# Sorted block attention and Fourier feed-forward: a trip through DRAM for mixed V, row stores without waits, norms by ln and exp, unread matmuls

## The chip, the cores and the metric

One core of a Trainium2 chip runs the whole program. The metric is the device time of one execution in microseconds. The kernel before takes 292.82 us (median of 3 runs, 292.41 to 292.87).

Five engines matter here: TensorE (PE in the profile), VectorE (DVE), ScalarE (ACT), GpSimd (POOL) and SyncE (SP, which here issues transfers only). Sixteen DMA engines move data beside them.

## The reference, cut to what matters

```python
def _attn_ref(q, k, v, sort_net):            # q, k, v: 4 x 8 x 768 x 64
    P = sort_net                             # 4 x 8 x 8 x 8
    for _ in range(5):
        P = np.exp(P - max); P = P / rowsum; P = P / columnsum
    k_sorted = einsum('bhij,bhjcd->bhicd', P, k_b)   # blocks of 96 keys are mixed
    v_sorted = einsum('bhij,bhjcd->bhicd', P, v_b)
    attn = softmax over the keys of a block of (q_b @ k_sorted.T / 8)
    return attn @ v_sorted

def _moe_ref(x, w1, w2):                     # x: 4 x 768 x 512
    u = x + real(fft2(x))
    un = (u - mean) / sqrt(var + 1e-6)
    return u + relu(un @ w1) @ w2            # 512 -> 2048 -> 512
```

V has to be mixed between blocks (contraction over block and head, 128 rows at a time) and must then lie with keys on partitions for attention times V. That turn is what the change does in another way.

## The kernel before

The kernel is written as a list of operations with costs, which a planner puts in a fixed order for each engine before the program is built. Two halves of V (t = 0 for batches 0 and 1, t = 1 for 2 and 3) go through the same code. V is loaded in long pieces, summed over keys on PE, reordered on VectorE and ScalarE into `vcx`, mixed by 64 small matmuls per half, whose output already has keys on partitions, and evicted with a stride into `vsf`:

```python
load(nat[t] ..., vv[128 * t:128 * t + 128, 48 * hf:48 * hf + 48, :])   # 6144 B pieces
... nc.tensor.matmul(psm.ap, idh, nat[t][:, ...512 columns])           # 12: sum over keys
... copy(e, vcd[:, dr, :, 8 * hf:8 * hf + 8], src)                     # 8 reorderings
for dd in range(4):
    nc.tensor.matmul(o, vcx[:, 96 * d:96 * d + m], bd, ...)            # keys x (block, head)
copy(e, vsb[0:96, :, 4 * n:4 * n + 4], ps...)                          # 16 strided evictions
```

Residual rows `u` live in six buffers of 128 x 512. A buffer is free again only when the store of its rows has landed. Rows of the first half of a sequence are stored by SP, the others by GpSimd with an indirect store:

```python
if T < 2:
    nc.sync.dma_start(out[b, t0:t0 + 128, :], u.ap)
elif T == 2:                                   # three stores: 112 rows, 15 rows, row 0
    ...
else:
    nc.gpsimd.indirect_dma_start(out..., rows[:, i:i + 1], u.ap)
```

The softmax here doesn't subtract the row's maximum and nothing guards it: scores larger than these inputs give would overflow.

Of the kernel before, what the change touches and what calls it, by code (L numbers as in the profile page):

```python
# [27 lines left out]
LOOK = {}  # L28
QB = (2, 3)
# [14 lines left out]
GT = 384  # L44


def _consts():
# [56 lines left out]
    vrow = np.zeros((1, 128, D + 1), f16)  # L104
# [9 lines left out]
    def as32(m):  # L114
# [8 lines left out]
                rows=rows, erow=np.tile(erow, (1, 4)), vrow=vrow, pack=pack)  # L123


class Op:
    __slots__ = ("n", "costs", "fn", "preds", "succs", "left", "ready", "prio",
                 "vts", "fresh", "nbytes", "end", "start", "eng", "tag",
                 "crit", "late")
# [13 lines left out]
class Plan:  # L143
# [14 lines left out]
    def add(self, costs, fn, r=(), w=(), prio=None, nbytes=0, tag="",  # L158
            after=()):
# [7 lines left out]
        o.preds, o.succs, o.vts, o.fresh = set(after), [], [], []  # L167
        for k in r:
            o.preds.update(self.wr.get(k, ()))
# [41 lines left out]
    def schedule(self):  # L211
# [48 lines left out]
        while todo:  # L260
# [70 lines left out]
            for s in o.succs:  # L331
                s.left -= 1
                for x in s.costs:
                    s.ready[x] = max(s.ready[x],
                                     o.end + (0.03 if x == e else self.XL))
                if s.left == 0:
                    for x in s.costs:
                        avail[x].append(s)
# [27 lines left out]
def kernel(  # L366
# [22 lines left out]
    def many(name, n, shape, dtype):  # L389
# [18 lines left out]
    vcx = ct("vcx", [128, 128 * D + 2], F16)  # L408
    dtab = vcx[:, 6144:7168].rearrange("p (c w) -> p c w", c=4)
    lt = vcx[0:97, 7168:7168 + LTW]  # L410
    vsf = ct("vsf", [97, 128 * (D + 1)], F16)
    vsb = vsf[:, 0:128 * (D + 1)].rearrange("p (g w) -> p g w", w=D + 1)
    eb4 = ct("eb4", [97, 4, EW], F16)
    P.pool("eb", [eb4[:, n, :] for n in range(4)])
# [14 lines left out]
    many("un", 2, [128, DM], F16)  # L429
# [9 lines left out]
             vcx[:, 7938:8194].bitcast(F32).rearrange(  # L439
# [3 lines left out]
    vbn = ct("vbn", [128, D], F16)  # L443
    rows = ct("rows", [128, 3 * B], mybir.dt.uint32)
    negone = ct("negone", [128, 1], F32)
    mhalf = ct("mhalf", [128, 3], F32)
    mone = ct("mone", [128, 3], F32)
# [7 lines left out]
    pk = hr[1].rearrange("p a b -> p (a b)")[0:32, 0:1024].rearrange(  # L455
        "p (i x) -> p i x", i=NB)
    pv = hr[1].rearrange("p a b -> p (a b)")[0:32, 1024:3072].bitcast(
        F32).rearrange("p (i x) -> p i x", i=NB)
    pws = hr[1].rearrange("p a b -> p (a b)")[0:32, 3072:3232].bitcast(F32)
# [9 lines left out]
    def load(dst, src, nbytes, w, prio, eng="POOL", r=(), after=()):  # L469
        e = {"POOL": nc.gpsimd, "SP": nc.sync}[eng]  # L470
        c = (0.8, 0.8) if eng == "POOL" else (0.1, 2.3)
        o = P.add({eng: c}, lambda _: e.dma_start(dst, src), r=r, w=w,  # L472
                  prio=prio, nbytes=nbytes, tag="load", after=after)
        o.late = 4.0 if after else 0.0
        return o


    slot = {}
# [34 lines left out]
    def load_v(t, hf, prio):  # L513
        load(nat[t].rearrange("p (c d) -> p c d", d=D)[
            :, 48 * hf:48 * hf + 48, :],
            vv[128 * t:128 * t + 128, 48 * hf:48 * hf + 48, :], 1572864,
            [("nat", t, hf)] + (hk(0)[8 * hf:8 * hf + 8] if t == 0 else
                                kqk(2 * hf) + kqk(2 * hf + 1)), prio)
# [10 lines left out]
    for n in range(4):  # L529
        P.add({"POOL": (1.5, 1.6)}, lambda _, n=n: nc.gpsimd.memset(  # L530
            eb4[0:96, n, :], 0.0), w=[("ebz", n)], prio=-190.0, tag="ebz")
# [8 lines left out]
    for t_, val in ((negone, -1.0), (mhalf, -0.5), (mone, 1.0)):  # L540
        P.add({"POOL": (0.1, 0.4)}, lambda _, t_=t_, val=val:
              nc.gpsimd.memset(t_, val), w=["smalls"], prio=-199.0, tag="small")
    P.add({"POOL": (0.9, 0.9)}, lambda _: nc.gpsimd.tensor_tensor(
        mone, mone, mhalf, op=ALU.pow), r=["smalls"], w=["mone"], prio=-198.0,
        tag="small")
# [5 lines left out]
            "o (n s) -> o n s", n=4), 13376),  # L551
        vrow=(vsf[96:97, 0:128 * (D + 1)], cn["vrow"].ap(), 16640),
# [14 lines left out]
    load_qk("k", 0, 0, -5000.0)  # L567
    load_qk("q", 0, 0, -4999.0)
    load_v(0, 0, -4998.0)
    load_v(0, 1, -4997.0)  # L570
    load_qk("k", 0, 1, -4996.0)
    load_qk("q", 0, 1, -4995.0)
    load_c("dtab", -4994.0)
    load_c("lt", -4993.0)
    load_c("cs", 19.0)
    load_c("tab", 20.0)
    for c in range(4):
        load_w1(c, 40.0 + c)
    for hf in range(2):
        load_qk("k", 1, hf, 30.0 + hf)  # L580
        load_qk("q", 1, hf, 30.5 + hf)
    for c in range(4):
        load_w2(c, 50.0 + c)
# [4 lines left out]
    V = nc.vector  # L588

    exps = []  # L590

    def sk(c, fn):
        o = P.add(c, fn, r=["pw", "rs"] + hk(1), w=["pw", "rs"], tag="sink")
# [3 lines left out]
    for it in range(5):  # L597
# [16 lines left out]
        sk({"DVE": (0.21, 0.21)}, lambda _: V.tensor_tensor(  # L614
# [6 lines left out]
        r=["pw"], w=["pk"] + hk(1), tag="pk")  # L621
    P.add({"ACT": (1.0, 1.05)}, lambda _: nc.scalar.copy(
        pv.rearrange("p i (g j) -> p i g j", j=NB),
        pw[:, :, None, :].broadcast_to([32, NB, 16, NB])),
        r=["pw"], w=["pv"] + hk(1), tag="pv")
# [6 lines left out]
    P.add(pe(0.45), f, r=["pk", "pack"] + hk(1), w=[bk], tag="psk")  # L632
# [35 lines left out]
    def v_path(t):  # L668
        n3 = nat[t].rearrange("p (c d) -> p c d", d=D)
        psm = Buf("pm", "pf") if t else Buf("pm")  # L670
        stage = [i for n in range(4) for i in kqk(n)] if t else hk(0)
        for hf in range(2):
            def f(_, hf=hf):
                for n in range(6):
                    nc.tensor.matmul(
                        psm.ap, idh,
                        nat[t][:, 3072 * hf + 512 * n:3072 * hf + 512 * n
                               + 512], start=(hf == 0 and n == 0),
                        stop=(hf == 1 and n == 5))
            P.add(pe(mm(512, 6) * (1.0 if t else 1.2)), f,  # L680
                  r=[("nat", t, hf), "pack"] + (
                      stage if t else stage[8 * hf:8 * hf + 8]), w=[psm], tag="psm")
        P.add({"DVE": (0.6, 0.68)}, lambda _: V.tensor_reduce(
            vb[:, 0, :], psm.ap.rearrange("p (c d) -> p d c", d=D),
            axis=AX.X, op=ALU.add), r=[psm], w=["vb"], tag="vb")
# [8 lines left out]
        vcd = vcx[:, 0:6144].rearrange("p (d r c) -> p d r c", r=6, c=16)  # L694
        for n in range(8):
            qd, hf = divmod(n, 2)
            dr = slice(16 * qd, 16 * qd + 16)
            src = n3[:, 48 * hf:48 * hf + 48, dr].rearrange(
                "p (c r) d -> p d r c", r=6)
            dst = vcd[:, dr, :, 8 * hf:8 * hf + 8]  # L700
            if t == 0:
                P.add({"DVE": dve(768), "ACT": act(768, 0.75)},
                      lambda e, dst=dst, src=src: copy(e, dst, src),
                      r=[("nat", 0, hf)] + stage[8 * hf:8 * hf + 8],
                      w=[("vcx", n)], tag="vcp")
            else:
                P.add({"DVE": dve(768, 1.0, 0.55)},
                      lambda _, dst=dst, src=src, dr=dr: V.tensor_tensor(  # L708
                          dst, src, vbn[:, dr, None, None].broadcast_to(
# [672 lines left out]
```

## Time and profile before

| what | before |
|---|---|
| median time | 292.82 us |
| span of the profiled run | 290.0 us |
| first feed-forward matmul (the hand-over) | 70.25 us |
| end of the last matmul | 281.46 us |
| tail after it | 8.5 us |
| mean granted clock of PE (the share of full speed that PE's clock was given) | 0.981 |

Up to the hand-over VectorE is full and PE waits; after it PE is full. The prediction below shows the lines. The timeline columns are start, duration, engine, line, operation, output and input.

```profile
7.52 6.17 POOL L530 MEMSET eb<- 96x1672 f16 x4
...
15.03 0.67 DVE L618 CAST hr<-hr 32x1024 f16<-32x1024 f32 x1
```

GpSimd's zero fills of the exponentials' buffers end at 13.69, and VectorE's conversion of the permutation comes after them, at 15.03, and takes 0.67 us. The second is from the DMA part: packets of all queues by size, then one group of transfers (how many, size of each, median time from issue to landing):

```profile
DMA packets 42529, 26.33 MB, mean 91 GB/s; under 512 B 30106, under 2 KB 38824, under 8 KB 42500
...
kq<-in_v_dram POOLq DMA_DIRECT2D x2, 768.0 KB, 21.5
```

The second half of V comes in two transfers.

### The profile page before, as it was taken

The numbers are of one execution on the slowest core, as the hardware profiler recorded it, in microseconds if no ns is written. First come the engines' busy times: TensorE is split into PE (matmuls) and PEld (weight loads), VectorE is DVE, ScalarE is ACT, GpSimd is POOL, SyncE is SP. The second block draws the span as 40 slices with busy tenths as digits, with TensorE's granted clock in tenths as the row PEclk, the third lists the DMA queues.
The fourth block names the chain that finished last, engine by engine and source line by source line (L and its number), as shares of the span: only waits on it lengthen the run. The fifth ranks groups of instructions, "written<-read, shape, count | busy, mean of one in ns | idle before, by whom it ended". The sixth has DMA issues, their size and how long they took to land.

```text
span 290.0 us, 5807 instructions
## 1 busy us (share of the span) xinstructions
PE 260.9 (90%) x2284; PEld 155.2 (54%) x2284; DVE 171.9 (59%) x405; ACT 157.9 (54%) x323; POOL 66.3 (23%) x104
## 2 busy tenths in 40 slices
PE   0389988897999999999999999999999999999980
PEld 0258866554565656554566456455555546545530
DVE  4697999999999999831579643145034226210020
ACT  2677979785778945970477037137415505425300
POOL 8973300015900640011220002032000212200021
PEclk9997999998899999999999999999999999999997
DMA  7999999910990897211113010311311111221001
GB/s 114 211 260 245 215 208 211 219 37 5 157 146 10 95 165 133 66 37 20 77 47 57 36 52 22 58 72 50 57 72 37 38 54 72 38 90 36 2 36 72
DMA packets 42529, 26.33 MB, mean 91 GB/s; under 512 B 30106, under 2 KB 38824, under 8 KB 42500
## 3 DMA queue, kind: packets, MB, share of 16 engines
q0 software_dynamic: 23536, 18.31, 37.4%
q1 hardware_dynamic: 18966, 7.64, 11.6%
q8 instruction: 18, 0.29, 0.4%
q14 instruction: 9, 0.07, 0.1%
HBM read 28.96 MB, written 6.29 MB: 122 GB/s over the span
## 4 chain that ended last, share of the span: by engine, by line
PE 62%; DVE 22%; DMA 8%; issue 3%; POOL 2%; ACT 1%; POOLq 0%; DVEq 0%
PE bank L1253 26%; PE bank L1274 25%; DMA hr<-in_v_dram 4%; DVE vsf L660 3%; DVE vcx L708 3%; DVE rt L1006 3%; DMA out_dram<-u,rows 2%; POOL kq L472 2%; DMA kq<-in_q_dram 2%; PE bank L1149 2%; PE bank L991 2%; DVE st L1186 1%; PE bank L952 1%; PE bank L897 1%; DVE ks L660 1%
## 5 line engine op out<-in xcount | busy, mean ns | idle before, releaser
L1265 ACT ACTIVATE hr<-bank 128x384 f16<-128x384 f32 x115 | 56.3, 491 | 75.2 <-PE bank L1253 74.4
L1253 PE MATMUL bank<-ut,w1sb 128*128 128x384 f16 x512 | 92.8, 329 | 0.7 <-ACT ut L660 0.7
L1274 PE MATMUL bank<-w2sb,hr 128*128 128x512 f16 x384 | 87.9, 379 | 0.0
L1253 PEld LDWEIGHTS <-w1sb 128*128 128x128 f16 x512 | 49.0, 99 | 34.8 <-issue 1.8
L1274 PEld LDWEIGHTS <-hr 128*128 128x128 f16 x384 | 36.7, 98 | 41.8 <-issue 0.2
L1282 DVE TENSOR_TENSOR u<-bank,u 128x512 f32<-128x512 f32 x24 | 16.5, 689 | 60.2 <-PE bank L1274 59.8
L961 ACT ACTIVATE ex<-bank 96x384 f32<-96x384 f32 x64 | 27.9, 485 | 6.3 <-PE bank L952 6.0
L1295 POOL DMA_INDIRECT out_dram<-u,rows x12 | 12.2, 1013 | 77.0 <-DVE u L1282 56.7
L1193 POOL TENSOR_SCALAR mv<-mv 128x3 f32<-128x3 f32 x8 | 1.9, 240 | 109.8 <-DVE mv L1188 109.8
L976 ACT ACTIVATE eb<-ex,negone 96x384 f16<-96x384 f32 x35 | 20.8, 615 | 0.2
L1213 ACT ACTIVATE un<-u,nm,ny 128x512 f16<-128x512 f32 x15 | 12.2, 810 | 11.8 <-DMA ut<-un 8.5
L1172 DVE SCALAR_TENSOR_TENSOR u<-rt,bank 128x510 f32<-128x510 f16 x12 | 8.1, 678 | 16.3 <-PE bank L1138 8.9
L991 PE MATMUL bank<-vsf,eb 97*128 97x65 f16 x416 | 16.5, 193 | 1.3 <-DVE rr L836 0.5
L1006 DVE TENSOR_TENSOR rt<-bank,rz 128x384 f16<-128x384 f32 x32 | 17.2, 549 | 0.3
L991 PEld LDWEIGHTS <-eb 97*128 97x128 f16 x416 | 15.4, 98 | 3.6 <-issue 1.3
L472 POOL DMA_DIRECT2D kq<-in_q_dram x20 | 16.4, 850 | 1.7 <-DMA kq<-in_q_dram 1.2
L1186 DVE BATCH_NORM_STATS2 st<-u 128x6 f32<-128x512 f32 x24 | 16.1, 686 | 0.3
L1160 DVE SCALAR_TENSOR_TENSOR u<-rt,bank 128x512 f32<-128x512 f16 x12 | 8.0, 684 | 13.9 <-PE bank L1153 13.5
L927 PE MATMUL bank<-pack,qr 128*128 128x128 f16 x48 | 4.8, 246 | 12.3 <-ACT qr L660 11.7
L724 PE MATMUL bank<-bdv,vcx 128*128 128x128 f16 (+1 forms) x128 | 12.6, 225 | 0.0
L952 PE MATMUL bank<-qt,ks 64*128 64x96 f16 x256 | 11.3, 207 | 1.3 <-DVE rt L1006 0.4
L897 PE MATMUL bank<-bdk,kq 128*64 128x128 f16 x192 | 10.7, 228 | 1.6 <-DVE bdk L636 0.8
(130 smaller groups left out, 338.2 us busy)
## 6 DMA issues: line engine op xcount, KB each, us to landing
kq<-in_k_dram POOLq DMA_DIRECT2D x8, 384.0 KB, 6.6
w1sb<-in_moe_w_ch_dram POOLq DMA_DIRECT2D x4, 512.0 KB, 16.0
w2sb<-in_moe_w_ch_dram POOLq DMA_DIRECT2D x4, 512.0 KB, 19.0
out_dram<-u SPq DMA_DIRECT2D x8, 256.0 KB, 2.0
kq<-in_q_dram POOLq DMA_DIRECT2D x4, 384.0 KB, 11.6
hr<-in_v_dram POOLq DMA_DIRECT2D x2, 768.0 KB, 11.2
kq<-in_v_dram POOLq DMA_DIRECT2D x2, 768.0 KB, 21.5
kq<-in_q_dram POOLq DMA_DIRECT2D x16, 96.0 KB, 5.5
```

Source lines behind the costliest of these rows:

```text
L472: o = P.add({eng: c}, lambda _: e.dma_start(dst, src), r=r, w=w, prio=prio, nbytes=nbytes, tag="load", after=after)
L897: nc.tensor.matmul(ps.ap[64 * h2:64 * h2 + 64, 128 * r3:128 * r3 + 128], k16[:, 2 * hl + h2, 3 * half + r3, :], bdk[:, 2 * hp + h2].rearra ...
L952: nc.tensor.matmul(pss[h2].ap[:, BLK * j:BLK * j + BLK], ks.ap[rows, 4 * g + j, :], qt.ap[rows, c0:c0 + BLK])
L961: nc.scalar.activation(ex.ap, pss[h2].ap[0:96, 0:384], AF.Exp, scale=SCALE),
L976: nc.scalar.activation(ed, src, AF.Identity, bias=negone[0:96])
L991: nc.tensor.matmul(po.ap[:, 65 * T:65 * T + 65], eb.ap[:, e0:e0 + 128], vsf[:, vi:vi + 65], start=(n == 0), stop=(n == len(WIN[T]) - 1), s ...
L1006: P.add({"DVE": (0.45, 0.56)}, lambda _: V.tensor_tensor(rt.ap[:, :, D * h:D * h + D], po3()[:, :, 0:D], rz.ap[:, :, None].broadcast_to([1 ...
L1186: P.add({"DVE": (0.6, 0.69)}, lambda _, u=u, st=st: V.bn_stats(st.ap, u.ap), r=[u], w=[st], tag="bn")
L1253: nc.tensor.matmul(ps.ap[:, 0:GT], w1sb[:, c, 128 * fc:128 * fc + 128], ut.ap[:, c, :], start=(c == 0), stop=(c == 3))
L1265: nc.scalar.activation(hr[g][:, fc, :], ps.ap[:, 0:GT], AF.Relu)
L1274: nc.tensor.matmul(ps.ap, hr[g][:, fc, 128 * tt:128 * tt + 128], w2sb[:, fc, :], start=(fc == 0), stop=(fc == 15))
L1282: V.tensor_tensor(u.ap, ps.ap, u.ap, op=ALU.add),
```

## The change

The intent: free VectorE and ScalarE before the hand-over (V needs no reordering and no strided eviction if a DMA does the turn), shorten the tail, keep PE's clock up with matmuls whose results nobody reads (unread matmuls). The core of the diff, cut:

```diff
 def load_v(t, hf, prio):            # second half of V
+        for r in range(3 * hf, 3 * hf + 3):
+            load(nat[1][:, 1024 * r:1024 * r + 1024].rearrange("p (c d) -> p c d", d=D),
+                vv[128:256].rearrange("p (c r) d -> p r c d", r=6)[:, r], ...)
 def v_path(t):                      # its sum moves from PE to VectorE
+        if t:
+            for n in range(4):
+                V.tensor_reduce(vb[:, 0, 16 * n:16 * n + 16],
+                    n3.rearrange("p c d -> p d c")[:, 16 * n:16 * n + 16], ...)   # planned 1.65 us
 def v_mix(t):                       # 12 wide matmuls, contiguous evictions, trip through DRAM
-                    nc.tensor.matmul(o, vcx[:, 96 * d:96 * d + m], bd, ...)
-                      e, vsb[0:96, :, 4 * n:4 * n + 4], ...
+                nc.tensor.matmul(o, bd, n4[:, r, 8 * hf:8 * hf + 8], ...)
+                      e, vm[:, 512 * n:512 * n + 512], ps.ap
+        for hb in range(2):
+            for k_ in range(3):
+                ....dma_start(vdr[t][w64, cols], vm[w64, cols])                   # 256 KB store
+                nc.gpsimd.dma_start(vsb[32 * k_:32 * k_ + 32, w64, 0:D],
+                    vdr[t][w64, cols].rearrange("g (c d) -> c g d", d=D))         # gather
 # exponentials: six buffers instead of four
+    for n in range(NEB):
+        P.add({"DVE": (1.0, 1.1)} if n < 2 else {"POOL": (1.5, 1.6)}, ... memset(eb4[0:96, n, :], 0.0))
 # norms: 1/sqrt by ln and exp on ScalarE instead of a chain on GpSimd (cut)
 # row stores
+                for x in st_:
+                    for y in stores if T < 3 else stores + direct:
+                        tc.declare_no_dep(x.ins, y.ins, reason="each row stored once")
 # unread matmuls in PE's planned gaps up to the hand-over
+                    for _ in range(int((o.start - t - 0.05) / SPIN)):
+                        nc.tensor.matmul(spin.ap[:, 0:480], idh, pack.bitcast(F16))
-    load_c("tab", 20.0)
+    load_c("tab", ...)              # ahead of K of batch 1
```

The order of many other operations changes too, because everything is planned anew.

## The prediction

> **What bounds the kernel now.** I read the busy shares in 40 slices first, then the chain that ended last, then stretches of ten and two microseconds, then the last ten microseconds by instruction.
>
> ```profile
> PE   0389988897999999999999999999999999999980
> DVE  4697999999999999831579643145034226210020
> PEclk9997999998899999999999999999999999999997
> ```
>
> DVE is full in slices 4 to 16 (about 30 to 115 us), PE from about 70 us to 280. The two clock dips, near 22 and 72 us, matter below.
>
> ```profile
> 3.55 12.80 DMA hr<-in_v_dram
> ...
> 20.05 0.36 PE bank L897 x6
> ...
> 31.11 2.75 DVE vsf L660 x4
> ...
> 69.61 0.59 ACT ut L660
> 70.25 2.14 PE bank L1253 x8
> ```
>
> The chain (start, duration, what) waits for V until 16.4 us, then goes through DVE and ACT evictions until the first feed-forward matmul at 70.25. I call that point the hand-over. After it I counted PE's instructions from 110 to 282 us and multiplied by warm spacings read off the chain (4 of L1253 in 0.65 us, 4 of L1274 in 0.86, 26 of L991 in 0.80, 4 of L1149 in 0.44): 448 x 0.1625 + 344 x 0.216 + about 23 us of smaller groups = 170 us of work in 172. The same count over 70.25 to 110 gives some 39 us in 39.75. So after the hand-over PE is the bound, and the span is three terms: hand-over (70.25) + PE's remaining work (211.2, to 281.46) + tail (8.5).
>
> ```profile
> 22.00:24.00 2.00, 2.00 (x28) 1.66 (x29) 1.79 (x5) 1.83 (x7) 1.07 (x3) 0.78 1.10 323
> 24.00:26.00 2.00, 2.00 (x26) 1.46 (x24) 1.30 (x4) 0.98 (x2) 0.53 (x1) 0.50 1.31 203
> 40.00:50.00 10.00, 7.91 (x160) 6.35 (x159) 9.97 (x28) 9.57 (x22) 0.00 (x0) 1.00 1.21 207
> 70.00:72.00 2.00, 1.75 (x8) 0.99 (x8) 1.87 (x6) 1.23 (x3) 1.85 (x4) 0.72 0.00 0
> 72.00:74.00 2.00, 2.00 (x12) 1.16 (x10) 1.67 (x3) 1.27 (x4) 2.00 (x3) 0.50 0.57 52
> ```
>
> Each row: stretch, length, busy PE, PEld, DVE, ACT, POOL, then granted clock, DMA share, GB/s. From 40 to 50 us both evicting engines are full (9.97 and 9.57 of 10). The clock is down at 22 to 26, while V is mixed, and again right at the hand-over.
>
> ```profile
> 278.12 0.69 DVE L1282 TENSOR_TENSOR u<-bank,u 128x512 f32<-128x512 f32 x1 [0.19 <-PE bank L1274]
> 278.22 1.09 POOL L1295 DMA_INDIRECT out_dram<-u,rows  x1 [29.14 <-DVE u L1282]
> 281.57 0.69 DVE L1282 TENSOR_TENSOR u<-bank,u 128x512 f32<-128x512 f32 x1 [2.76 <-PE bank L1274]
> 281.86 0.97 POOL L1295 DMA_INDIRECT out_dram<-u,rows  x1 [2.55 <-DMA out_dram<-u,rows]
> 285.36 0.96 POOL L1295 DMA_INDIRECT out_dram<-u,rows  x1 [2.52 <-DMA out_dram<-u,rows]
> ```
>
> The second and third row stores of the last group are each held until the one before has landed; their data were ready at 278.81 and 282.26.
>
> **What the Trainium skill says.** *TensorE: Matmul & The Clock Gate*, Part 1 (the HAM clock gate): the array runs at 1.2 GHz after about one idle window of 3.4 us and at 2.4 GHz after a busy one. The trace agrees: the first six matmuls that sum V take 2.77 us together, the next six 1.46, and the stretch at 24 us has clock 0.50. *DMA: Bandwidth & Descriptors*, Anatomy of one DMA: about 2.0 us fixed per transfer; here an indirect store lands a median 2.7 us after issue. The same page, Specifications: line rate needs pieces of at least 512 B; the gather of mixed V moves 128 B pieces, which nothing in this trace times. *ScalarE: Activation LUTs*, Table sets: exp and ln share the set natural_log_exp_and_others, one load. The trace has one table load of 1.28 us; that no second appears is for the changed profile to show.
>
> **The change, part by part.**
>
> *Mixed V, first half (before the hand-over).* Removed: eight reorderings of V (5 on DVE of 941 ns, 3 on ACT of 1499: 9.2 us) and 16 strided evictions (774 to 791 ns; 11.5 us of the 23.0 in both halves). Added: 12 contiguous evictions of 512 columns. ACT's copy of 128x512 from PSUM took 586 ns and DVE's 64x512 cast 684, so 12 x 0.63 = 7.6 us. Added also: two memsets moved from POOL to DVE (my estimate 1.4 us, from 336 ns for a 768-column f16 copy) and a second expansion of the permutation (1.04, as L622 took). Net 10.7 us less on two engines that are both full: 5.3 us each. PE loses 128 small matmuls and gets 24 of 512 columns; at 22 to 28 us it was on the chain with clocks of 0.78, 0.50 and 0.87, a loss of 2 x (0.22 + 0.50 + 0.13) = 1.7 us which the unread matmuls should save. Together 7.0 us.
>
> A check by the other road, the arrival of mixed V. V goes first: 3.15 of the 4.7 MB that had come by 16.37 us, so 3.55 + 12.8 x 0.67 = 12.1 us. Sum, mean and bdv then end near 15, PE and evictions near 20.5. Store (2.3 to 3 us), then three gathers. If a 128 B piece costs what the plan of the change assumes (1.7 us per gather), V is back near 29 us, against 35 now (last eviction at 34.20, 0.79 long). That is 6 us, consistent with 7. The batch-0 scores, exponentials and their evictions (about 24 us on two engines) fill the wait, and six instead of four buffers for exponentials let them.
>
> *Norms by ln and exp.* The POOL chain from 64.33 to the first normalised row at 66.21 is 1.9 us, on the chain. Two small ACT operations and one DVE operation I put at 0.7 with their hops. Gain 1.2 us. The seven later norms lie beside full PE: nothing.
>
> *Unread matmuls up to the hand-over.* Keep the clock up at 70 to 74 us, where PE has just become the bound: 2 x 0.28 + 2 x 0.50 = 1.5 us.
>
> *Mixed V, second half.* DVE loses 8 x 1.473 us, PE trades 64 x 0.055 for 12 x 0.216: 0.9 us off PE's remaining work. The relief of DVE (some 7 us of both engines together) lies beside a full PE.
>
> *Stores without waits.* The third store starts at 282.3 instead of 285.36: 3.1 us off the tail. Elsewhere the waits (10.1 us of POOL, 5.5 of DVE for u buffers) are beside PE.
>
> *Loads moved.* The row-bias table is small and its consumer is fed before the hand-over anyway: 0.
>
> *Paid back.* Before 70.25 the present kernel has also done all of batch 1's attention on PE, about 9 us (96 / 2 x 0.0485 + 128 / 2 x 0.035 + 104 x 0.031 + 24 x 0.055). With an earlier hand-over part is left for later. But the same work costs 15 us per evicting engine, so leaving it also brings the hand-over forward; I book 0.5 us net loss.
>
> Sum: 7.0 + 1.2 + 1.5 + 0.9 + 3.1 - 0.5 = 13.2 us. 292.8 - 13.2 = 279.6; I state 279.
>
> **The rivals.** First: the gather is slow. The present hardware queue takes 11.6% x 290 x 16 / 18966 = 28 ns per packet (mean 403 B). At that price 6144 pieces over 16 engines are 10.8 us, V is back at about 34 us, and weights and tables queue behind. Then the 7.0 us shrinks to 1 to 2 and the time is about 285. For it: DMA is full (share above 1) until 58 us already, and POOL waits in order. Against it: 128 B pieces are smaller than that queue's mean, and the weights are not needed until the hand-over. Second: much more is gained. With V early and critical work first, the hand-over could come at 52 to 55 us, since evictions of batch 1 that now interleave (DVE 9.9 of 10 from 37 to 69) are pushed behind it; then 270. For it: 9 us of PE against 15 per evicting engine. Against it: the present order interleaves the same way, and w1 lands only after the gated loads. Third: the second half of V comes too late for batch 2 and PE, which issues in order, stalls in the middle. Its load is cut to 256 B pieces and it makes a trip to DRAM; but PE has two feed-forward groups of about 20.7 us each and batch 1 to do first. A stall of 5 us would make 284. Fourth: the unread matmuls delay real ones; with a misjudged gap a few tenths each, 1 to 2 us.
>
> **Range and chances.** The tail (3.1) and the norms and clock (2.7) are nearly certain; the front varies between +1 and +15. That gives 271 to 286 for 8 in 10. Two per cent is 287.0: faster 0.91, within 0.07, slower 0.02.
>
> **What would show it.** Right: first L1253-type matmul near 61 to 63 us; PE full after it; the last three indirect stores each within 1.2 us of their residual add; end some 5.5 us after the last matmul; no clock dip at the hand-over; first attention-times-V matmul near 29 us; one table load. Wrong: attention-times-V held by the gather past 33 us, PE idle between 80 and 130 us with V of batches 2 and 3 as releaser, the hand-over waiting for w1, or a hand-over before 56 us.

## The result

The changed kernel takes 302.32 us (median of 4 runs, 301.91 to 303.51); the kernel before in the same rounds took 292.62. The ratio is 1.0343 (95% interval 1.0307 to 1.0379): slower by 3.4%, where 279.0 us was predicted. A single-core run is called slow when it is over 1.5% above the fastest of the same kernel. Ratios here and below are the mean time of one kernel's fast runs over that of the other's of the same rounds, so not quite the ratio of the quoted medians; those of the experiments leave out the profiled run (that of e18 also takes in a slow run, see there).

The busy shares of the changed kernel in 40 slices of 7.5 us:

```profile
PE   5769898989995992999799999999999999999992
DVE  6878989999879891768569934415505414612010
PEclk9959999999999798699989999999999999999998
DMA  7995899999999389999930201122111121021102
```

PE now has holes at slices 13 (about 94 us), 16 (about 117) and 20 (about 147), each followed by a dip of the clock. The DMA engines are busy in nearly all of slices 1 to 20 (to 150 us; slice 14 has 3 tenths); before, they are at 3 tenths or less from slice 17 (116 us) on. The timeline gives the first attention-times-V matmul and the hand-over:

```profile
41.70 1.35 PE L1071 MATMUL bank<-vsf,eb 97*128 97x65 f16 x39
...
68.70 1.47 PE L1332 MATMUL bank<-ut,w1sb 128*128 128x384 f16 x8
```

The hand-over was predicted at 61 to 63, attention times V near 29. Stretches of it follow (length, then busy PE, PEld, DVE, ACT, POOL, clock, DMA share, GB/s):

```profile
22.00:24.00 2.00, 2.00 (x26) 1.47 (x21) 1.04 (x5) 1.65 (x4) 0.00 (x0) 0.69 1.31 206
70.00:72.00 2.00, 2.00 (x26) 1.10 (x25) 1.97 (x8) 2.00 (x5) 2.00 (x1) 1.00 1.29 206
72.00:74.00 2.00, 2.00 (x30) 1.55 (x29) 2.00 (x6) 1.92 (x6) 0.91 (x2) 1.00 1.96 172
94.00:98.00 4.00, 0.82 (x5) 0.29 (x3) 3.96 (x7) 0.49 (x1) 0.00 (x0) 1.00 0.40 57
114.00:118.00 4.00, 1.05 (x7) 0.49 (x6) 0.00 (x0) 1.42 (x4) 3.09 (x4) 1.00 1.05 185
146.00:150.00 4.00, 1.91 (x13) 0.67 (x13) 2.93 (x7) 0.49 (x1) 0.75 (x1) 0.94 0.88 115
```

The clock dip at the hand-over is gone, as intended. The three holes are different from one another: at 94 VectorE is full, at 114 VectorE has nothing to do at all. The chain of what ended last, in these stretches (start, duration, what):

```profile
93.28 2.72 DVE vb L714
96.00 0.60 DVE u L1361
...
111.88 8.24 DMA out_dram<-u
120.30 0.70 DVE u L1244
121.04 0.50 PE bank L1032 x8
...
140.51 6.46 DMA out_dram<-u,rows
```

The first hole stands behind L714, the sum of the second half of V, which VectorE does in order before the feed-forward's residual add L1361. The second and third stand behind stores of rows of `u`, which take 8.24 and 6.46 us to land; such stores land a median 1.9 to 2.7 us after issue in the kernel before. Their buffers are waited for. At the second hole it is the end of a tile's rows, stored in small transfers of 15 rows (30 KB) and of one row (2 KB): for the 15 rows the profile gives 8.3 us at the longest, against 1.9 before. At the third hole (store under way from 140.5 to 147.0) the trip itself is over: its last gather was issued at 115.74 and none took longer than 19.7 us. What loads the DMA engines then are loads of K and Q, which GpSimd issues behind the gathers; it waited for their landing before this one:

```profile
130.91 0.82 POOL L487 DMA_DIRECT2D kq<-in_q_dram  x1 [7.23 <-DMA vsf<-vdr]
```

It issued the last of these loads at 138.6; in e9 below, with a small trip, all were issued by 120. The DMA part:

```profile
DMA packets 56545, 32.61 MB, mean 108 GB/s; under 512 B 42843, under 2 KB 51561, under 8 KB 56517
...
vsf<-vdr POOLq DMA_DIRECT2D x12, 256.0 KB, 11.0
...
kq<-in_v_dram POOLq DMA_DIRECT2D x6, 256.0 KB, 17.3
```

Packets under 512 B rose by 12,737. Six loads of 256 KB in pieces of one key (128 B of f16 in SBUF, 256 B of f32 in DRAM) are 6 x 2048 = 12,288, nearly all of it: so these would be the loads of the second half of V, every sixth key, and not the gathers (e6 tests it). And the fronts of both kernels differ in one more thing:

```profile
10.94 6.10 POOL L568 MEMSET eb<- 96x1672 f16 x4
...
12.08 5.51 DVE L651 CAST fo<-rv 32x1024 f16<-32x1024 f32 x1
```

The same conversion that took 0.67 us now takes 5.51, beside the fills. It is on the way to the sum of V, whose second half starts only at 17.97 us. The tail is as predicted:

```profile
292.80 0.69 DVE L1361 TENSOR_TENSOR u<-bank,u 128x512 f32<-128x512 f32 x1 [0.18 <-PE bank L1353]
292.90 0.96 POOL L1376 DMA_INDIRECT out_dram<-u,rows  x1 [35.69 <-DVE u L1361]
294.16 0.96 POOL L1376 DMA_INDIRECT out_dram<-u,rows  x1 [0.19 <-issue]
...
297.21 0.96 POOL L1376 DMA_INDIRECT out_dram<-u,rows  x1 [1.97 <-DVE u L1361]
```

To compare all kernels I use one account of each profiled run. Span = hand-over + PE's work after it + what PE loses after it + tail. Work is the prediction's count: matmuls in the trace at the warm spacing (384 columns in 162.5 ns, 512 in 216, others in proportion, at least 31 ns, four times the columns for f32). Lost is the rest up to the end of the last matmul: idle time and cold clock. The count is good to about 1 us. The hand-over itself differs by up to 2 us between chips with the front as it was (70.25 to 72.02 below).

| kernel | hand-over | work after | lost | tail | span |
|---|---|---|---|---|---|
| before | 70.25 | 209.7 | 1.5 | 8.5 | 290.0 |
| changed | 68.70 | 211.2 | 16.2 | 5.6 | 301.7 |

So 14.7 us more are lost on PE after the hand-over, 1.5 more are done there, and the hand-over and the tail give back 1.5 and 3.0: the difference of 11.7 us.

### The profile page after: what moved, and what is told of

Read it like the earlier page. It is cut to its first block, busy times and chain, and to the rows that moved or that the text cites. A ratio compares the mean times of both kernels' runs of the same rounds, so it can differ in the third digit from the quotient of the medians.

```text
span 301.7 us, 5644 instructions
## 1 busy us (share of the span) xinstructions
PE 272.8 (90%) x2197; PEld 151.6 (50%) x2197; DVE 182.7 (61%) x426; ACT 143.3 (47%) x313; POOL 77.3 (26%) x106
## 2 busy tenths in 40 slices
DMA packets 56545, 32.61 MB, mean 108 GB/s; under 512 B 42843, under 2 KB 51561, under 8 KB 56517
## 3 DMA queue, kind: packets, MB, share of 16 engines
q0 software_dynamic: 37312, 23.82, 54.0%
## 4 chain that ended last, share of the span: by engine, by line
issue 47%; PE 20%; DVE 19%; DMA 7%; POOL 4%; ACT 1%; SPq 1%; POOLq 0%; DVEq 0%
PE bank L1353 4%; PE bank L1332 4%; POOL out_dram L1376 3%; DVE rt L1087 3%; DMA out_dram<-u 3%; DMA out_dram<-u,rows 2%; DVE fo L651 2%; PE bank L770 2%; DMA vcx<-k_dtab 2%; PE bank L977 2%; DVE pmt L1104 1%; PE bank L1144 1%; DVE st L1270 1%; DVE eb L1054 1%; DVE u L1361 1%
## 5 line engine op out<-in xcount | busy, mean ns | idle before, releaser
L1332 PE MATMUL bank<-ut,w1sb 128*128 128x384 f16 x512 | 94.0, 331 | 4.7 <-DVE u L1361 4.7
L1344 ACT ACTIVATE hr<-bank 128x384 f16<-128x384 f32 x104 | 51.0, 491 | 88.7 <-PE bank L1332 87.7
L1353 PE MATMUL bank<-w2sb,hr 128*128 128x512 f16 x384 | 90.4, 385 | 0.0
L1361 DVE TENSOR_TENSOR u<-bank,u 128x512 f32<-128x512 f32 x24 | 16.5, 689 | 57.9 <-PE bank L1353 57.7
L487 POOL DMA_DIRECT2D kq<-in_q_dram x20 | 16.2, 813 | 23.9 <-DMA vsf<-vdr 11.4
L1462 PE MATMUL bank<-pack 128*128 128x480 f16 x73 | 18.2, 389 | 3.3 <-DMA pack<-k_pack 3.3
L1056 ACT ACTIVATE eb<-ex,negone 96x384 f16<-96x384 f32 x34 | 20.0, 612 | 0.2
L1032 PE MATMUL bank<-qt,ks 64*128 64x96 f16 x256 | 12.4, 211 | 7.1 <-DVE u L1244 6.0
L798 POOL DMA_DIRECT2D vsf<-vdr x12 | 12.8, 1068 | 14.8 <-DMA vdr<-hr 13.2
L1341 DVE TENSOR_SCALAR hr<-bank 128x384 f16<-128x384 f32 x24 | 13.3, 555 | 4.5 <-PE bank L1332 4.3
L1032 PEld LDWEIGHTS <-ks 64*128 64x128 f16 x256 | 7.4, 96 | 15.4 <-issue 13.7
L714 DVE TENSOR_REDUCE vb<-kq 128x16 f32<-128x1536 f16 x4 | 10.8, 2774 | 2.9 <-DMA kq<-in_q_dram 2.9
## 6 DMA issues: line engine op xcount, KB each, us to landing
w2sb<-in_moe_w_ch_dram POOLq DMA_DIRECT2D x4, 512.0 KB, 19.7
kq<-in_v_dram POOLq DMA_DIRECT2D x6, 256.0 KB, 17.3
```

The lines of the kernel that those rows point to most:

```text
L1032: nc.tensor.matmul(pss[h2].ap[:, BLK * j:BLK * j + BLK], ks.ap[rows, 4 * g + j, :], qt.ap[rows, c0:c0 + BLK])
L1056: nc.scalar.activation(ed, src, AF.Identity, bias=negone[0:96])
L1332: nc.tensor.matmul(ps.ap[:, 0:GT], w1sb[:, c, 128 * fc:128 * fc + 128], ut.ap[:, c, :], start=(c == 0), stop=(c == 3))
L1344: nc.scalar.activation(hr[g][:, fc, :], ps.ap[:, 0:GT], AF.Relu)
L1353: nc.tensor.matmul(ps.ap, hr[g][:, fc, 128 * tt:128 * tt + 128], w2sb[:, fc, :], start=(fc == 0), stop=(fc == 15))
L1361: V.tensor_tensor(u.ap, ps.ap, u.ap, op=ALU.add),
```

## The experiments

Eighteen kernels ran. Except for e8, e13, e14, e16 and the pair e17 and e18, which were planned anew, the edit was made after planning, so that every engine kept the order of its instructions. The theory: four costs were misjudged (zero fills that hold VectorE, small pieces, long sums, the trip through DRAM) and the other parts of the change work. The rivals: the unread matmuls delay real ones, or the gather's small pieces are the whole cost, or PE loses its time in other ways.

The account of the runs that are argued from, with the ratio to the kernel before:

| run | hand-over | work after | lost | ratio |
|---|---|---|---|---|
| e1 replica of the change | 67.28 | 211.2 | 19.7 | 1.0425 |
| e2 gathers in 4 KB pieces | 70.44 | 211.2 | 7.6 | 1.0088 |
| e5 fills on ScalarE | 64.11 | 211.2 | 16.9 | 1.0266 |
| e3 half sums | 68.93 | 211.2 | 9.9 | 1.0172 |
| e6 loads in 2 KB pieces | 68.52 | 211.2 | 14.0 | 1.0191 |
| e4 = e1 + e2 + e3 | 69.04 | 211.2 | 6.9 | 0.9984 |
| e10 = e3 + e5 + e6 | 63.68 | 211.2 | 13.9 | 1.0084 |
| e15 small gathers | 67.03 | 211.2 | 9.3 | 1.0041 |
| e9 small trip | 68.60 | 211.2 | 3.0 | 0.9936 |
| e11 = e9 + e10 | 66.22 | 211.2 | -0.8 | 0.9633 |
| e12 before, stores | 72.02 | 209.7 | 1.2 | 0.9868 |
| e16 before, unread matmuls | 71.20 | 209.7 | 0.7 | 1.0005 |
| e8 before, all but V | 71.30 | 209.7 | 0.2 | 0.9877 |
| e13 first half of V only | 66.18 | 214.9 | 3.3 | 0.9950 |
| e17 six buffers of u | 66.03 | 211.3 | 13.0 | 1.0164 |
| e18 nine buffers of u | 65.82 | 211.3 | 8.5 | 1.0183 |

### e1: zero fills later in the order

```diff
+        fills = [o for o in order if o.tag == "ebz" and o.eng == "POOL"]
+        order = [o for o in order if o not in fills]
+        at_ = max(n for n, o in enumerate(order) if o.tag == "pv") + 1
+        order[at_:at_] = fills
```

> The changed kernel with every engine's instructions in the same order, except that GpSimd's four zero fills (6.1 us) come after the conversions of the permutation instead of beside them. Theory (VectorE's conversion L651, 5.51 us instead of 0.67, was held by the zero fills[...]): L651 takes 0.6 to 0.8 us, the second half of the sum of V starts 3 to 5 us earlier than 17.97, first attention-times-V at 36 to 39 instead of 41.7, hand-over at 64 to 67 instead of 68.7, time 297 to 301 (302.3 now; the later stalls swallow a part). Rival A (the slow gather alone sets the hand-over and the end): L651 short again but first attention-times-V still after 40 and the time within 1.5 us of 302.3. Rival B (L651 was slow for another reason, e.g. waiting data): it still takes over 3 us.

305.69 us (304.18 to 306.19), ratio 1.0425. The edit did nothing: GpSimd had no work between, so the fills ran at 10.85 us as ever, and L651 took 5.42 us. The run is a replica of the change, and shows how far two copies lie apart on different chips: 1.034 and 1.043 in time, 16.2 and 19.7 us lost, hand-overs at 68.70 and 67.28. A difference of two single profiles is good to no better than that.

### e2: gathers in pieces of 4 KB

```diff
-                              vsb[32 * k_:32 * k_ + 32, w64, 0:D],
-                              vdr[t][w64, cols].rearrange("g (c d) -> c g d", d=D)
+                              vsf[32 * k_:32 * k_ + 32, 64 * VW * hb:64 * VW * hb + 4096] ...
+                              vdr[t][w64, cols].rearrange("(p a) x -> p a x", a=2)
```

> The changed kernel with the same order, but each of the twelve gathers of mixed V moves its 256 KB in pieces of 4 KB instead of 128 B (wrong result on purpose; a fill of the ones' column on GpSimd becomes one of the gaps on VectorE). Theory (2048 pieces of 128 B per gather occupy the DMA engines: landing 11 us in the median): landing of these twelve falls to 3 to 6 us, packets of the software queue fall from 37312 to about 13500, first attention-times-V at 35 to 38 instead of 41.7, the waits for the store of u at 112 to 120 and at 141 to 147 shrink from 8.2 and 6.5 us to under 4, time 292 to 297. Rival (the pieces are not the cost; stores and waits of the new round trip are): landing stays over 8 us and the time stays within 2 us of 302.3.

296.19 us (293.76 to 296.52), ratio 1.0088; the result is wrong on purpose, as wherever that is said below. The time fell as much as the theory said, but not by its mechanism. Packets under 512 B stayed at 42,842 and those of the software queue at 37,312: the gathers had never been recorded as packets of 128 B, so I had miscounted them. Their landing only fell from 11.0 to 9.2 us. GpSimd's issue of one fell from 1.07 to 0.55 us, and the edit had also moved a fill to VectorE, so that the conversion began later and took 3.10 us. That last cannot be the gain: the conversion ended only 0.67 us earlier and the hand-over came at 70.44, later than in the change. All of the gain lies after it, where PE lost 7.6 us instead of 16.2 with the same bytes on the trip. Whether the pieces or the shorter issue gave it is open.

### e3: half the sum

```diff
-                    n3.rearrange("p c d -> p d c")[:, 16 * n:16 * n + 16],
+                    n3.rearrange("p c d -> p d c")[:, 16 * n:16 * n + 16, 0:BLK // 2],
```

> The changed kernel with the same order, but VectorE's four reductions that sum the second half of V (L714, 2.77 us each, planned as 1.65) read only half of the keys (wrong result on purpose). Theory (this reduction holds back, in order, the evictions of the feed-forward and so PE at 94 to 97 us and its clock after): 1.4 us each, the idle of PE at 94 to 97 gone or under 1 us, clock at 98 to 102 back at 1.0, time 297.5 to 300. Rival (loads of V arriving at 85 us are the cause): the stall shrinks by less than 1 us and the time stays within 1 us of 302.3.

298.45 us (296.48 to 305.26, one of them slow), ratio 1.0172. The four sums take 1.46 us instead of 2.77, PE is full from 94 to 98, and it loses 9.9 us instead of 16.2. That is more than the first hole alone: the second remains (PE idles 6.3 us behind L1245, the add that waits for a buffer of `u`), but of the third, near 147, only a wait of 1.4 us is left.

### e4: the three edits at once

e1 + e2 + e3.

> The three edits together: zero fills moved, big pieces, half reductions. Theory (these three misjudged costs are what turned the gain into a loss): hand-over at 60 to 64 us, no idle of PE over 2 us between hand-over and end, time 280 to 287, that is what was predicted for the change. Rival (the unread matmuls, the extra evictions or a lasting cold clock take the rest): hand-over early but PE's work after it still over 220 us, time over 290.

294.07 us (290.84 to 298.49), ratio 0.9984: a miss, for 280 to 287 was expected. The hand-over stayed at 69.04, for the fills still ran beside the conversion, and PE still idled 6.0 us behind the store of `u`.

### e5: fills on ScalarE

```diff
+        halves = [lambda e, n=n, h=h: nc.scalar.copy(eb4[0:96, n, 836 * h:836 * h + 836],
+                                                     eb4[0:96, 0, 836 * h:836 * h + 836]) ...]
+        # one after each of ScalarE's five exponentials of the permutation, GpSimd's fills taken out
```

> The changed kernel, same order, with GpSimd's four zero fills done instead as eight copies of zeros on ScalarE, in the gaps that it has in the first 13 us (run e1 had moved them in the order only, and they ran at the same time, so it tested nothing). Theory (VectorE's conversion L651 cannot run while GpSimd fills; it ended 0.55 us after the last fill in the profiles of the change, of e1 and of e2): L651 takes 0.6 to 0.8 us instead of 5.5 and ends before 13.5; second half of the sum of V at 13 to 15 instead of 17.97; first attention-times-V at 36 to 39 instead of 41.7; hand-over 64 to 67 instead of 68.7; ratio to the kernel before 1.020 to 1.034 (1.0343 and 1.0425 measured for the change and its replica e1). Rival (loads or the gather set the front): L651 short, but first attention-times-V after 40 and the ratio over 1.034.

300.18 us (299.59 to 301.46), ratio 1.0266, as the theory said. The timeline of e5:

```profile
10.23 0.87 ACT L1461 COPY eb<-eb 96x836 f16<-96x836 f16 x1
12.07 0.68 DVE L651 CAST fo<-rv 32x1024 f16<-32x1024 f32 x1
...
64.11 1.47 PE L1332 MATMUL bank<-ut,w1sb 128*128 128x384 f16 x8
```

The conversion takes 0.68 us with nothing else changed on VectorE, so the fills had held it. Attention times V starts at 37.01 instead of 41.70 and the hand-over comes 4.6 us earlier (3.2 against the replica); of it 2.3 us show in the time (1.0266 against 1.0343). *SBUF — State Buffer*, section "Who interferes with whom", says why such a thing can be: VectorE and GpSimd share a pair of ports, a VectorE copy or cast may take it, and the loser waits wholly. The traces agree: L651 ended 0.55 us after the last fill in the change (17.59 against 17.04), in e1 (17.51 against 16.95) and in e2 (16.92 against 16.37), wherever it had begun. The kernel before shows it too: its copy of V at 12.92 took 1.32 us where the next took 0.80, and ended at 14.24, 0.55 after the last fill. PE's loss stays at 16.9.

### e6: the second half of V in pieces of 2 KB

```diff
-                vv[128:256].rearrange("p (c r) d -> p r c d", r=6)[:, r], 690000,
+                vv[128:256, 16 * r:16 * r + 16, :], 690000,
```

> The changed kernel, same order, but the six loads of the second half of V read 16 consecutive keys (pieces of 2 KB) instead of every sixth key (pieces of 128 B); the result is wrong on purpose. Theory (these 12288 pieces of 128 B are what was added to the packets under 512 B, 30106 to 42843, and together with the gathers of Q in pieces of 128 B they hold the DMA engines at a share over 2 from 70 to 90 us): packets under 512 B fall back to about 30600, the share at 80 to 90 falls from 2.06 to under 1.3, these loads land in under 10 us instead of 17.3, VectorE's sum L714 starts before 80 instead of at 85.15, and the first stall of PE (94 to 97) shrinks; ratio 1.015 to 1.030. Rival (VectorE's long reductions and the later gather stall PE whatever the loads do): share falls, but the ratio stays over 1.032.

299.24 us (296.74 to 301.10), ratio 1.0191 (1.0130 to 1.0252).

```profile
DMA packets 45024, 32.61 MB, mean 109 GB/s; under 512 B 30554, under 2 KB 39272, under 8 KB 44996
```

The 12,288 small packets are gone, which shows whose they were. The DMA share at 70 to 80 us falls from 2.10 to 1.16. But the loads still take 15.8 us to land instead of 17.3, the share at 80 to 90 is still 1.96, and the sum L714 starts at 83.03 instead of 85.15, where I had expected before 80. The Q loads in 128 B pieces, which the kernel before has too, fall in the same time; that they are what is left was not tested. The profiled run lost 2.2 us less than the change, but it is the slowest of the four: by the times the edit gave 4.4 us (1.0191 against 1.0343).

### e7: without the unread matmuls

```diff
-                        nc.tensor.matmul(spin.ap[:, 0:480], idh, pack.bitcast(F16))
+                        pass
```

> The changed kernel without its 73 unread matmuls, order otherwise the same. If they delay real matmuls (rival four of the prediction): hand-over 1 to 2 us earlier, ratio 1.028 to 1.034. If they do what they are for: clock lower than 0.82 and 0.84 in 10 to 30 us, hand-over 1 to 3 us later, ratio 1.036 to 1.050. If they do nothing, within 0.3% of 1.0343 to 1.0425.

302.58 us (300.75 to 306.69, two of five slow), ratio 1.0324 (1.0277 to 1.0371), beside 1.0343 and 1.0425 of the change and its replica. It lies in the range stated for a delay as well as in that for no effect, so a delay of a microsecond or two is not excluded; a loss of 10 us by them is, and no gain shows.

### e8: everything but the new way of V

The kernel before with the stores, the norms, the unread matmuls and the table's earlier load, planned anew.

> The kernel before with every part of the change except the new way of mixing V: row stores that do not wait, norms by ln and exp, unread matmuls, row-bias table ahead of K of batch 1. By the prediction's terms: 3.1 + 1.2 + 1.5 = 5.8 us, a ratio of 0.980 (0.975 to 0.985). Theory (all of the loss comes with the new way of V): ratio under 0.99. Rival (the unread matmuls or the re-planned order lose): ratio over 1.0.

289.15 us (288.50 to 289.62), ratio 0.9877 (0.9838 to 0.9915). It is correct and beats both kernels, though by 1.2% where the prediction's terms made 2.0. It was planned anew, so its parts cannot be told apart here; but all of the loss lies with V.

### e9: a small trip for the second half

```diff
+            few = slice(64 * hb, 64 * hb + (8 if t else 64))
-                          vdr[t][w64, cols], vm[w64, cols]),
+                          vdr[t][few, cols], vm[few, cols]),      # and the gather likewise
```

> The changed kernel, same order, where the second half of mixed V makes its trip through DRAM with 8 of 64 rows per transfer (32 KB instead of 256 KB, six stores and six gathers; wrong result on purpose). Theory (these 3 MB keep the DMA engines busy from 105 to 120 us and so a store of u takes 8.2 us to land instead of 2, VectorE waits for its buffer and PE for VectorE, 6.0 us): the landing of that store falls under 3.5 us, the idle of PE at 115 to 121 falls under 1.5 us, ratio 1.005 to 1.022 (1.034 and 1.043 measured for the change). Rival (the three small stores of one row tile, or the issue of transposes in the same queue, delay it): landing stays over 5 us, ratio over 1.03.

290.31 us (289.95 to 293.85), ratio 0.9936, better than the 1.005 to 1.022 expected. PE loses 3.0 us instead of 16.2. The same stretches as above, of e9:

```profile
94.00:98.00 4.00, 1.23 (x6) 0.39 (x4) 3.96 (x7) 0.45 (x1) 0.00 (x0) 1.00 0.29 54
114.00:118.00 4.00, 4.00 (x45) 2.27 (x42) 3.82 (x9) 3.74 (x10) 4.00 (x6) 1.00 1.67 158
```

The first hole is still there, the second (and the third) are gone, with the cold clock after them. No store of rows takes more than 3.3 us to land, against 8.3 in the change; of e9, over all stores of rows:

```profile
DMA to landing us min/median/max: 1.9/2.7/3.3
```

The trip of the second half, 1.5 MB out and 1.5 MB back beside PE's full time, costs 13 us of PE's time by these two profiles, 12 by the times. *DMA: Bandwidth & Descriptors*, section "Queues, rings and completion order", fits: each DMA engine takes turns between the queues that have work, a packet at a time, so a small store shares its engines with what else is queued. The trace shows the landing, 8.24 us beside the trip, but not the turns: that they are the reason is not shown.

### e10: fills, loads and sums mended, the trip in full

e3 + e5 + e6.

> Three of the mended costs together: zero fills on ScalarE (e5), 2 KB pieces for the load of the second half of V (e6), half reductions (e3); the trip through DRAM in full; wrong result on purpose. Theory: hand-over at 63 to 65 us, no stall of PE at 90 to 100, the stall of about 6 us behind the store of u still there; ratio 0.992 to 1.012. Rival (gains do not add, since the later stall grows as the earlier ones shrink): ratio over 1.015.

295.73 us (295.11 to 297.13), ratio 1.0084. Hand-over at 63.68 and no hole at 90 to 100, as expected. But PE still loses 13.9 us, with waits of 3.6 us at 108 and 5.1 us at 141, both behind buffers of `u`, one store of which takes 8.79 us to land. What the earlier hand-over and the shorter sums give is in part taken there: 5.2 us earlier than e3, and 4.0 us more lost.

### e11: all four mended

e9 + e10.

> The same three, and the short trip through DRAM of e9 as well; wrong result on purpose. Theory (front, sum, loads and trip are the whole of the difference from the prediction): hand-over at 63 to 65, PE full after it, 64 + 211 + 5.5 = 281 us and up to 4 us of small stalls, ratio 0.955 to 0.975. Rival (PE has lost its time to something else, such as a colder clock or longer evictions): ratio over 0.985 with PE's idle after the hand-over still over 8 us.

283.03 us (281.20 to 284.39), ratio 0.9633 (0.9559 to 0.9708), as expected; the hand-over at 66.22 was not (63 to 65 expected, 63.68 in e10, for a reason not known). PE's shares in e11:

```profile
PE   5989896999999999999999999999999999999992
```

No hole is left and the loss is nil by the account. The four costs make up 19 of the 23 us between the change (302) and the prediction (279); the 4 that stay are the hand-over, predicted at 61 to 63. It is no kernel to use, for its results are wrong: it skips work, and so bounds what mending could give.

### e12: the stores alone

The kernel before, same order, with the diff of the row stores only.

> The kernel before, same order, with the stores of rows not waiting for one another and nothing else. Prediction's term: 3.1 us off the tail, ratio 0.987 to 0.992; last matmul at the same time, end 5.4 us after it instead of 8.5. Rival (the three indirect stores contend and land no earlier): ratio over 0.996.

289.84 us (288.81 to 290.51), ratio 0.9868 (0.9808 to 0.9928). The tail is 5.77 us instead of 8.54. It does what e8 does, within the intervals.

### e13 and e14: the first half the new way, the second the old way

```diff
-NEB = 6
+NEB = 4
+    vcd = ct("vcd", [128, 3072], F16)     # reordering of the second half in two rounds
+        # t == 1: load_v, sum on PE, reordering, 64 small matmuls and strided evictions as before
```

> A new, correct kernel, planned anew: everything of the change for the first half of V, but the second half of V loaded, summed, reordered and evicted as the kernel before does (its reordering in two rounds through a buffer of half the size; four buffers for exponentials instead of six). Theory (all of the loss lies in the second half's loads, sums and trip, the first half's way gains): hand-over at 62 to 67 us, no stall of PE over 2 us after it, ratio 0.962 to 0.982, better than 0.988 of the kernel before with the other parts alone. Rival (the first half's way gains nothing either, its relief falls on ScalarE which is not full): hand-over over 68, ratio 0.984 to 1.0.

> The kernel of e13, same order, with GpSimd's two remaining zero fills done on ScalarE. Theory: as e13 or up to 2 us faster (two fills hold VectorE's conversion for 3 us at most). Rival (the fills no longer meet the conversion in this plan): within 0.4% of e13.

291.23 us (290.35 to 291.67), ratio 0.9950, and 291.05 (290.06 to 291.73), ratio 0.9947; both correct. My theory missed: 0.962 to 0.982 was expected. The hand-over does come at 66.18, 5.1 us before that of e8, but 5.2 us more of PE's work then lie behind it (214.9 against 209.7) and 3.1 more are lost. The work is the same in sum; it has moved: four heads' attention of batch 1 (260 - 208 = 52 matmuls of attention times V at 31 ns), some scores, and the sum of the second half of V on PE (12 x 0.216 = 2.6 us). So an earlier hand-over, by itself, is no gain. The two fills on ScalarE shortened the conversion from 3.04 to 0.68 us in e14 and moved the time by nothing.

### e15: small gathers, full stores

> The changed kernel, same order, with only the gathers of the second half of V cut to 8 of 64 rows; its stores of 256 KB stay (wrong result on purpose). If gathers alone delay the store of u: its landing under 4 us and a ratio near e9's 0.994. If the stores to DRAM do as much: landing 4 to 6 us and a ratio of 1.005 to 1.02. If the stores alone: ratio over 1.025.

294.50 us (291.61 to 294.89), ratio 1.0041. PE loses 9.3, between e9's 3.0 and the 16.2 of the change, and the store of `u` in the second hole lands in 4.89 us instead of 8.24 (4 to 6 us and 1.005 to 1.02 were stated for this case): both legs of the trip delay others, the stores about as much as the gathers. With one profile each, a finer split is not to be had.

### e16: the unread matmuls alone

> The kernel before, same order, with the unread matmuls up to the hand-over and nothing else. Prediction's term: 1.7 us (mixing of V no longer at clocks of 0.78 and 0.50) and 1.5 us (clock at 70 to 74 us), ratio 0.988 to 0.995. Rival (they only fill idle time that was not on the path): ratio 0.997 to 1.003 with the clock up.

292.22 us (291.63 to 293.62), ratio 1.0005 (0.9947 to 1.0063). The clock at 70 to 80 us is 1.00, where e12, without them, has 0.83, and the loss after the hand-over is 0.7 us. But at 20 to 30 us, where V is mixed, the clock is 0.66, as in e12 without them (0.83 in the kernel before): it was not kept up there. No gain shows in the time. The order is not the same as before, though that was meant: the edit adds two entries and a PSUM buffer ahead of planning, and in the profile VectorE does 13 of the 32 strided evictions where it did 16. So a gain that the new plan took back is not excluded.

### e17 and e18: six and nine buffers of u

```diff
-NEB = 6
+NEB = 4
-    many("u", 6, [128, DM], F32)
+    more = [ct(f"u_{i}", [128, DM], F32) for i in range(9)]     # 6 in e17; fills on ScalarE in both
```

> The changed kernel, correct, planned with four buffers for exponentials instead of six, zero fills on ScalarE, six buffers of u. It is the control of e18. By both theories as e5: hand-over 63 to 68 us, 13 to 18 us lost on PE after it, ratio 1.01 to 1.035.

> The kernel of e17, same order, with nine buffers of u in the space that the two buffers for exponentials gave up. Theory (the trip of the second half through DRAM costs time only because the store of u lands late and its buffer is waited for): the waits of VectorE for stores of u of 3 to 7 us disappear, PE loses under 8 us after the hand-over, ratio 0.975 to 1.0. Rival (the trip slows Q and K loads of batches 2 and 3 as well, and PE waits for those): the waits move to those loads, ratio within 0.01 of e17.

297.53 us (295.69 to 298.92), ratio 1.0164, and 297.20 (292.92 to 299.33), ratio 1.0183; both correct. The waits, first of e17, then of e18 (who waits for what: us in total, times, longest):

```profile
DVE u L1245 <- DMA out_dram<-u: 6.8, 1, 6.8
```

```profile
PE bank L845 <- DVE vb L743: 4.9, 1, 4.9
```

In the profiled run of e18 VectorE's wait for a store of `u` is gone from the list, and PE's longest wait after the hand-over is one behind the sums of V; PE loses 8.5 us and not 13.0. Expected were under 8 us and a ratio under 1.0: a miss. And that run, 292.92 us, is the fastest of four; the other two fast ones took 297.2. The ratio 1.0183 leaves it out, as a profiled run, and takes in the slow one of 299.33; the three fast runs have a mean of 295.8 us, the four of e17 297.4. By the times there is no clear difference. So the wait for the buffer is one way in which the trip reaches PE, but whether the slower runs wait for other transfers instead is open. I have no profile of one.

## Why the prediction was wrong

The frame held: span = hand-over + PE's work + tail. What it left out was the fourth term, PE's loss after the hand-over, taken as nil in its sum and then only as a rival.

- **"Mixed V, first half ... Together 7.0 us."** Failed. The hand-over came 1.5 us earlier, with the norms' 1.2 and the clock included. Three things in its place. The conversion was held by the fills (5.51 us for 0.67), and that cost 4.6 us of hand-over (e5; 3.2 against the replica). The prediction itself listed the two fills moved to VectorE, but not that four remained on GpSimd and would slide beside VectorE's copies. Then the relief was booked as "5.3 us each", but it showed as idle time of ScalarE: busy time up to 70 us went from 52.4 to 42.1 there, and from 60.6 to 61.6 on VectorE, which stayed the full one (4.8 of it are the held conversion). Last, the check by the other road assumed the store and gather at 2.3 to 3 and 1.7 us behind nothing, some 8.5 us from the last eviction to attention times V; here it took 12.4 us (from 29.35), and 13.0 in e5 (from 23.99), and V was back at 41.70, not 29 (37.01 without the fills). What that part costs by itself was not tested.
- **"I book 0.5 us net loss"** for batch 1's work left behind the hand-over. Too small: in the change 52 matmuls of attention times V and 20 of scores more lay behind the hand-over, 2.4 us by the account, against 1.5 us by which the hand-over came earlier. In e13 as much of it, 2.6 us, and the sum of V on PE, 2.6, pay back all of 5.1.
- **"Mixed V, second half ... 0.9 us off PE's remaining work. The relief of DVE ... lies beside a full PE."** The 0.9 was right (1.5 more work after the hand-over is 2.4 less 0.9), but the step failed most by what it left out: it looked at PE's and VectorE's busy time only, and not at the transfers. The trip takes 13 us (e9), the sums on VectorE, which take 2.77 us each and not the planned 1.65, 6 us when measured alone (e3), and the two overlap (13 + 6 is more than the 14.7 lost). The third rival named the place ("80 and 130 us with V of batches 2 and 3 as releaser") but sized it at 5 us where 14.7 more were lost, and did not see that stores of `u` would be the ones to wait.
- **First rival, the slow gather.** Gathers were slow to land (11.0 us in the median), but for the most part not by its price per piece: with 4 KB pieces (e2) they still took 9.2 us, and the packets were as many.
- **"Unread matmuls ... 1.5 us" and 1.7 us, "Norms ... 1.2 us".** The dip at the hand-over went, as predicted, and the one table load of 1.28 us stayed the only one. But mixing still began at a clock of 0.69 (22 to 24 us), and e7 (1.0324), e16 (1.0005) and e8 against e12 (0.9877 and 0.9868) show no gain in time from these parts. One reading is less firm than it says: the first six matmuls of V's sum took 2.77 us while the recorded clock was 1.00 (12 to 16 us).
- **"Stores without waits ... 3.1 us."** Right: the tail fell by 3.0 us, and by 2.8 in e12, each indirect store within 1.2 us of its data.
- **Loads moved: 0.** Not tested apart from the rest of e8.

The kernel to use is the one before with the stores' part (e12, 289.84 us) or with all but V (e8, 289.15 us); the two are not told apart.

## What to carry to other kernels

A transfer that runs "beside a full engine" is only free if no small transfer that somebody waits for runs at the same time; look for the stores that free buffers, and ask what will be queued with them, and which loads the same engine will issue later for it. When work is taken from two engines, ask on which of them it will in fact fall, and what work an earlier hand-over merely leaves for later. A cost measured in one place holds only beside the same neighbours: the conversion of 0.67 us took eight times as long next to another engine's fills.

## What the Trainium skill lacked or had wrong

- *SBUF — State Buffer*, "Who interferes with whom": it says that whoever starts first has the ports for the whole instruction. Here VectorE's conversion, begun beside four fills in a row (1.59 us each), took 5.51 us for 0.68 alone and ended 0.55 us after the last of them, so it did not get in between. That a row of instructions can hold the other engine off is not said.
- *DMA: Bandwidth & Descriptors*, "Queues, rings and completion order": no figure is given for a small store beside a large transfer of another queue. Here a store of 15 rows (30 KB) took 8.3 us, for 1.9 in the kernel before, while the 3 MB of the trip's stores and gathers were under way.
- *DMA: Bandwidth & Descriptors*, "Specifications": it gives 512 B as the least for line rate, but the page does not say which pieces of a transfer share one packet, so a trace's small packets cannot be read as small pieces. Twelve gathers of 2,048 runs of 128 B each added none under 512 B (42,843, and 42,842 with 4 KB pieces, e2); six loads of as many pieces added 12,288 (e6).
- No page has the time of a VectorE sum over a strided f16 view (what the pages measure of hopping reads is for 32-bit streams): 128 x 1536 elements read with a stride of 128 B took 2.77 us, and 128 x 768 took 1.46.
